# Gated attention and SwiGLU on one core: scale arithmetic and weight copies to GpSimd, probability casts to ScalarE

## The chip, the core and the metric

The kernel runs on one core of a Trainium2 chip. The metric is device time in microseconds (us): three runs took 1774.62 to 1776.85, median 1776.02. Beside them there is one profiled execution, from which all rows come.

A core has five engines that matter here, each with a queue that it works through in order: TensorE (PE, with its weight loads PEld), VectorE (DVE), ScalarE (ACT), GpSimd (POOL) and SyncE (SP), which here issues the DMAs. They meet at semaphores. Matmul results lie in PSUM, in eight banks of 128 x 512 float32; everything else lies in SBUF.

## The reference

Two branches on the same input of 2048 rows and 576 columns are mixed by a gate:

```python
g = sigmoid((x * gate_w).sum(-1, keepdims=True))
a = A_ref(x, wq, wk, wv, wo, beta)                 # 32 heads of 18, 4 segments of 512 rows
b = (silu(x @ w_gate) * (x @ w_up)) @ w_down       # 576 -> 4608 -> 576
return g * a + (1 - g) * b
# inside A_ref, for each segment:
p = softmax(qs @ ks.T * scale + mask);  a_dot = p @ vs
a_mem = (phi(qs) @ M) / (phi(qs) @ z + 1e-6)       # memory of the segments before
o = sigmoid(beta) * a_mem + (1 - sigmoid(beta)) * a_dot
```

## The kernel before

**Stages.** First the attention's projections are made, segment by segment, with the memory terms (to 239 us in the trace). Then comes the feed-forward branch, in two *halves* of two segments each. A half goes through the 36 blocks of 128 hidden columns, f = 0 to 35; one block is called a *unit* here. Last, a tail mixes and projects (from about 1692 us).

**A unit.** Gate and up products of the block are made together by a scheme of seven products in place of eight: `seven(t, j)` issues seven matmuls of 128 x 512 (L1365, L1368), 49 a unit. ScalarE and VectorE combine their sums between them: L1444, L1447, L1454 and L1458 are copies by ScalarE, L1451 and L1459 additions by VectorE, L1461 and L1463 the SiLUs, L1469 and L1470 products that give the hidden values, L1243 and L1246 their split into two float16 parts. The three accumulators have one PSUM bank each (0, 1 and 2), so the fifth product, which adds on to the bank that L1451 reads, waits for L1451.

**Ticks.** Between the products `tick()` is called eight times, k = 0 to 7; ticks 5 and 6 follow each other with no product between them. A tick issues what is due (`defer(n, fn)` puts a small piece of work n ticks ahead; the pieces of the next block's weights, L358, L362, L366, are spread in this way), then down products and steps of attention by the table `SHARE`. The order of the program is the order of each queue: nothing is moved by a scheduler.

**Heavy units.** The down products are made for three blocks at a time (CH = 3), in the first unit of each group of three after the first group: f = 3, 6, ..., 33 of a half, called *heavy*. They are 16 groups of nine matmuls (L1144), in two PSUM banks in turn (3 and 4), each ended by VectorE (L1151, L1153), which multiplies by `inv[c]` and adds to `ya`. In half zero the steps of attention run in the heavy units alone, ten in each but the first, at ticks 2 to 7; in half one they run in all units. The two lighter units after a heavy one are called the second and the third.

**A step of attention** makes scores twice: by rows for the maxima (L882, then VectorE's L900, which reads a bank and writes a scratch tile `junk`), and by columns (L993), on which ScalarE does `exp` into `pe` (L997) and GpSimd masks the diagonal (L1005). Two steps later `pe` is split: L1092 casts it to float16 (`p1`, VectorE) and L1094 subtracts (`p2`, GpSimd). The value products (L1021, L1023) come later still. The tiles of PSUM for this come from `ts_tile`, three banks (5, 6, 7) in turn. In half one units of attention are made in a second way (`turned`), which has no L1092.

**Scales.** Everything is held in float16 pairs under scales that are powers of two, worked out in the kernel from sums of squares. `across` adds columns over partitions by a matmul against ones (L155). `grade` cuts at a floor and takes a power of two near the reciprocal root by two bit steps (L149, L151, L152).

- `weigh(i, t)` (L169 to L190) does so for four blocks of gate and up weights: 17 steps on VectorE, 19 for i < 2, on operands of one to eight columns. It gives `sw`, `iw`, `hk`, `ha`, `hb`. For i = 0 and 1 it runs in the first part, for i = 2 to 8 at tick 2 of a third unit.
- `d_scale(c)` (L1106 to L1120) does it for three blocks of down weights: eight or nine steps on VectorE and one or two multiplications on GpSimd (L1119). It runs at tick 0 of the second unit.
- `d_look(f)` (L1104) gives it the sums: ScalarE squares a down weight block and writes the squares to `junk` too. `d_load` brings the blocks in ticks 0 to 2 of the first unit of the three, `d_look` follows at ticks 4 to 6.
- `d_split(f)` (L1122 to L1129) makes three float16 copies of a block: the scaled one (ScalarE, L1125), the rest (VectorE, L1126), and the first one divided by 2048 (VectorE, L1127), and stores them for half one.

`exp_table` (L1358) is a tiny `exp` that makes ScalarE load its table early, after the SiLUs.

Of the kernel before, what the change touches and what calls it, by code (L numbers as in the profile page):

```python
# [17 lines left out]
AF = mybir.ActivationFunctionType  # L18
# [51 lines left out]
def gated_mix(ctx, tc, xT, xrest, wf, wfr, wfh, wd, wv, wo, beta, cmask, ident, bmask, out):  # L70
# [77 lines left out]
    def grade(out, t, low=FLOOR):  # L148
        nc.vector.tensor_scalar_max(out, t, low)  # L149
        bits = out.bitcast(I32)  # L150
        nc.vector.tensor_scalar(bits, bits, 24, 127, op0=OP.logical_shift_right, op1=OP.bitwise_xor)  # L151
        nc.vector.tensor_single_scalar(bits, bits, 23, OP.logical_shift_left)  # L152

# [15 lines left out]
    def weigh(i, t):  # L169
        c = 20 + 9 * i  # L170
        n = 9 if i < 2 else 8
        e, z, m = sc[:, 0:8], column(8), sc[:, 9:13]
        across(t[:, :n], sc[:, c:c + n])
        nc.vector.tensor_reduce(sw[i], t[:, :n], axis=AX.X, op=OP.add)
        grade(sw[i], sw[i])
        nc.vector.tensor_scalar_mul(sw[i], sw[i], TOP)
        nc.vector.tensor_scalar(e, t[:, 0:8], sw[i], sw[i], op0=OP.mult, op1=OP.mult)
        if i < 2:
            nc.vector.tensor_scalar(z, t[:, 8:9], sw[i], sw[i], op0=OP.mult, op1=OP.mult)
            nc.vector.tensor_scalar_add(e, e, z)  # L180
        v = e.rearrange("p (f u) -> p f u", u=2)
        nc.vector.tensor_mul(m, v[:, :, 0], v[:, :, 1])
        nc.vector.tensor_reduce(z, m, axis=AX.X, op=OP.max)
        nc.vector.tensor_mul(z, z, xq)
        grade(z, z, 2.0 ** 26)
        nc.vector.tensor_mul(iw[i], sw[i], sx)
        nc.vector.tensor_scalar(hk[i], z, 4.0 * STEP * TOP, iw[i], op0=OP.mult, op1=OP.mult)
        nc.vector.tensor_scalar(ha[i], hk[i], iw[i], 1.0 / STEP, op0=OP.mult, op1=OP.mult)
        nc.vector.reciprocal(hb[i], ha[i])
        nc.vector.reciprocal(iw[i], iw[i])  # L190
# [192 lines left out]
    with ExitStack() as st:  # L383
# [344 lines left out]
        for s in range(NSEG):  # L728
            upd = upd_gen(s - 1) if s else None
            casts = []  # L730
            for n, (m, u) in enumerate(chains):
# [18 lines left out]
                if s == 2:  # L750
                    if n == 6:
                        mid.append(lambda: weigh(1, lone_tile([P, 9])))
                    if n == 0:
# [40 lines left out]
            for n in range(8):  # L794
# [4 lines left out]
                if s == 1:  # L799
                    if n == 3:  # L800
                        power(sx, lone_tile([P, 1]))
                    if n == 4:
                        reach(lone_tile([P, 4 * NT]))
                    if n == 6:
                        weigh(0, lone_tile([P, 9]))
# [30 lines left out]
    with ExitStack() as st:  # L836
# [205 lines left out]
        def att_gen():  # L1042
            N = 10 * NB
            for tau in range(N + TL + VL + 5):
# [44 lines left out]
                if 0 <= z < N and z // 5 not in turned:  # L1089
                    pe = cur.pop(z)  # L1090
                    p1 = ap.tile([P, L], F16, name="p1", bufs=6)
                    nc.vector.tensor_copy(p1, pe)  # L1092
                    p2 = ap.tile([P, L], F16, name="p2", bufs=6)
                    nc.gpsimd.tensor_sub(p2, pe, p1)  # L1094
                    cur["p", z] = (p1, p2)
# [10 lines left out]
        def d_scale(c):  # L1106
            t, r = ts_tile([P, CH]), sc[:, 13:16]
            across(t, sc[:, 123:126])
# [8 lines left out]
            nc.vector.tensor_reduce(inv[c], r, axis=AX.X, op=OP.min)  # L1117
            for n, i in enumerate(at):
                nc.gpsimd.tensor_mul(column(121 + n), inv[c], hb[i])  # L1119
            nc.vector.reciprocal(inv[c], inv[c])  # L1120

        def d_split(f, r):  # L1122
# [4 lines left out]
            defer(3, lambda: nc.vector.tensor_scalar_mul(d[:, 2], d[:, 0], 1.0 / STEP))  # L1127
# [111 lines left out]
        later = [False]  # L1239
        yas = {}  # L1240
# [132 lines left out]
        for pos, (half, f) in enumerate(seq):  # L1373
# [22 lines left out]
            if half == 0 and pos % 3 == 2 and 2 <= i < FT // 4:  # L1396
                plan.append((2, lambda i=i: weigh(i, ts_tile([P, 8]))))
# [15 lines left out]
            def tick():  # L1413
# [5 lines left out]
                if half == 0:  # L1419
                    if q == 0 and k < CH:  # L1420
                        draw[f + k] = d_load(f + k)
                    if q == 0 and 4 <= k < 4 + CH:
                        d_look(f + k - 4)
                    if q == 1 and k == 0:
                        d_scale(f // CH)
                    if (q, k) in ((1, 1), (1, 7), (2, 5)):
                        g = f - 1 if k == 1 else f
# [8 lines left out]
            later[0] = half == 1 and f > 0  # L1436
            ops, rem = wops.pop((half, f)), rhs[f % 2]
# [151 lines left out]
```

## Time and profile before

| What | Value |
|---|---|
| Median of three runs | 1776.02 us |
| Profiled execution, its own time | 1776.07 us |
| Its span, first to last instruction | 1774.4 us |
| Granted TensorE clock, mean | 0.996 |
| DMA, mean | 175 GB/s |
| First part; half zero; half one; tail (us) | 239.4; 736.8; 716.3; 81.9 |

The span is 1.7 us shorter than the execution's time, which lies 0.05 us off the median, so a microsecond in the trace is taken as one in the result. The page gives busy times of each engine. A row of a timeline reads: start, duration, engine, line, operation, out<-in, shapes, count, and in brackets the idle time of the engine before it and what ended that. A row of waits reads: who waited at which line, for what, us in total, times, longest. A row of stretches gives the stretch, its length, and then the busy time of PE, PEld, DVE, ACT and POOL with counts, the granted clock, and the DMA. Matmuls overlap one another, so a row's duration is longer than the time to the next start.

### The profile page before, as it was taken

What the parts mean: (1) busy time and instruction counts of PE and PEld (TensorE: products, weight loads), DVE (VectorE), ACT (ScalarE), POOL (GpSimd) and SP (SyncE); (2) the same over time, 40 slices, a digit from 0 to 9 for tenths busy, and PEclk for the clock granted to TensorE, in tenths of its full rate; (3) what the DMA queues carried; (4) which work ended last, traced back from release to release, by engine and by line L of the source; (5) the groups of instructions that cost most, each with busy time, mean ns of one, the idle gap of its engine ahead of it and who ended that gap; (6) DMA issues with size and microseconds to landing.
All of it is one profiled execution on the core that took longest, in us unless ns stands there. A gap on an engine that the chain in (4) does not pass through costs nothing.

```text
span 1774.4 us, 35271 instructions
## 1 busy us (share of the span) xinstructions
PE 1688.2 (95%) x12267; PEld 1094.0 (62%) x12267; DVE 1392.2 (78%) x3467; ACT 1047.0 (59%) x1868; POOL 839.5 (47%) x1083
## 2 busy tenths in 40 slices
PE   9999989999999999889899999999999999999999
PEld 7888855445555555555555566566556656655599
DVE  7788667888898889888887787878778788786565
ACT  7656567676766676566555656655664665565411
POOL 3325551246356544644552474656555565554121
PEclk9999999999999999999999999999999999999999
DMA  8656666656765674455444557764866586665544
GB/s 288 212 211 219 225 212 217 206 165 180 230 209 157 204 223 154 134 165 179 118 125 158 156 128 155 199 158 124 189 177 137 151 214 165 142 147 142 155 148 141
DMA packets 341670, 311.30 MB, mean 175 GB/s; under 512 B 193396, under 2 KB 258676, under 8 KB 341492
## 3 DMA queue, kind: packets, MB, share of 16 engines
q1 hardware_dynamic: 341492, 309.05, 60.6%
q8 instruction: 96, 1.57, 0.4%
q14 instruction: 82, 0.67, 0.1%
HBM read 183.20 MB, written 99.55 MB: 159 GB/s over the span
## 4 chain that ended last, share of the span: by engine, by line
PE 55%; DVE 18%; ACT 10%; issue 9%; DMA 5%; POOL 3%; SPq 1%; DVEq 0%; ACTq 0%; POOLq 0%
PE bank L1365 20%; PE bank L1144 16%; PE bank L212 7%; PE bank L1368 3%; PE bank L882 3%; PE bank L993 2%; DVE ya L1153 2%; ACT L1461 2%; DVE junk L900 2%; DVE hl L1246 1%; DMA rc<-rt 1%; PE bank L1021 1%; ACT row L1463 1%; ACT L1358 1%; DVE p L1092 1%
## 5 line engine op out<-in xcount | busy, mean ns | idle before, releaser
L1144 PE MATMUL bank<-dw,hh 128*128 128x320 f16 (+1 forms) x2304 | 436.9, 286 | 25.9 <-DVE ya L1153 21.3
L1144 PE MATMUL bank<-dw,hl 128*128 128x320 f16 (+1 forms) x1152 | 329.9, 286 | 1.1 <-DVE hl L1246 1.1
L1094 POOL TENSOR_TENSOR p<-pe,p 128x512 f16<-128x512 f32 x220 | 270.8, 1231 | 86.6 <-DVE p L1092 62.5
L1144 PEld LDWEIGHTS <-hh 128*128 128x128 f16 x2304 | 224.5, 98 | 117.1 <-issue 31.3
L997 ACT ACTIVATE pe<-bank 128x512 f32<-128x512 f32 x220 | 130.1, 591 | 194.4 <-PE bank L993 183.0
L1153 DVE SCALAR_TENSOR_TENSOR ya<-bank,sc,ya 128x320 f32<-128x320 f32 x352 | 176.0, 511 | 60.9 <-PE bank L1144 58.5
L900 DVE CUSTOM_DVE_ANT_0 junk<-bank,cm 128x128 bf16<-128x128 f32 (+2 forms) x352 | 169.5, 481 | 32.6 <-ACT junk L1104 22.2
L1368 PE MATMUL bank<-xr,rh 128*128 128x512 f16 x504 | 191.4, 380 | 0.4 <-DMA rh<-rc 0.4
L1005 POOL TENSOR_SCALAR_AFFINE_SELECT pe<-pe 128x256 f32<-128x256 f32 (+1 forms) x220 | 91.8, 417 | 175.1 <-ACT pe L997 171.3
L1246 DVE SCALAR_TENSOR_TENSOR hl<-hh,row 128x512 f16<-128x512 f16 x144 | 124.1, 862 | 27.1 <-ACT hh L1243 27.0
L358 POOL TENSOR_TENSOR ws<-raw 128x256 f32<-128x256 f32 x72 | 66.3, 921 | 152.0 <-DMA raw<-in_wf_dram 104.5
L882 PE MATMUL bank<-kst,qst 108*128 108x512 bf16 (+3 forms) x512 | 124.6, 299 | 12.5 <-ACT pe L997 10.9
L1144 PEld LDWEIGHTS <-hl 128*128 128x128 f16 x1152 | 112.5, 98 | 30.8 <-DVE hl L1246 1.8
L1092 DVE CAST p<-pe 128x512 f16<-128x512 f32 x220 | 110.1, 501 | 0.0
L1454 ACT ACTIVATE row<-bank 128x512 f32<-128x512 f32 x72 | 43.0, 597 | 103.8 <-PE bank L1368 103.8
L993 PE MATMUL bank<-qst,kst 111*128 111x512 bf16 (+3 forms) x352 | 103.3, 300 | 0.6 <-DMA kst<-stw 0.6
L1458 ACT ACTIVATE bank<-bank 128x512 f32<-128x512 f32 x72 | 41.9, 582 | 100.2 <-PE bank L1368 98.3
L1459 DVE TENSOR_TENSOR row<-bank,row 128x512 f32<-128x512 f32 x72 | 49.7, 690 | 56.2 <-ACT bank L1458 55.9
L212 PE MATMUL bank<-xo,qhi 128*128 128x512 f32 x288 | 92.6, 402 | 0.1
L1243 ACT ACTIVATE hh<-row 128x512 f16<-128x512 f32 x144 | 89.1, 619 | 5.0 <-DVE row L1469 4.1
L456 POOL TENSOR_TENSOR q<-qr,q 128x512 bf16<-128x512 f32 x36 | 47.9, 1332 | 84.6 <-ACT q L455 75.6
L1469 DVE SCALAR_TENSOR_TENSOR row<-bank,sc,row 128x512 f32<-128x512 f32 x72 | 53.8, 748 | 42.4 <-ACT row L1461 20.5
(1089 smaller groups left out, 4195.7 us busy)
## 6 DMA issues: line engine op xcount, KB each, us to landing
xo<-in_wf_dram SPq DMA_DIRECT2D x65, 320.0 KB
raw<-in_wf_dram SPq DMA_DIRECT2D x72, 256.0 KB
dc<-dw SPq DMA_DIRECT2D x36, 432.0 KB
dw<-dc SPq DMA_DIRECT2D x36, 432.0 KB
rh<-rc SPq DMA_DIRECT2D x72, 168.0 KB
draw<-in_wd_dram SPq DMA_DIRECT2D x36, 288.0 KB
xo<-in_xT_dram SPq DMA_DIRECT2D x33, 256.0 KB
vd<-vps SPq DMA_DIRECT2D x8, 912.0 KB
```

The source lines that it names most:

```text
L212: nc.tensor.matmul(t, st[n], mv[n], start=(n == 0), stop=(n == 13))
L882: nc.tensor.matmul(t[:, c:c + w], qs[:KR, pr, P * i:P * i + P], ks[:KR, pr, 0:w], start=True, stop=True)
L900: nc.vector.tensor_tensor_reduce(junk.bitcast(BF)[:, :w], t[:, c:c + w], cm[:, L - w:L], 1.0, -3.0e38, OP.add, OP.max, m[:, k:k + 1])
L993: nc.tensor.matmul(t[:, c:c + w], ks[:KR + 3, pr, P * j:P * j + P], qs[:KR + 3, pr, P * j:L], start=True, stop=True)
L997: nc.scalar.activation(pe, t, AF.Exp, scale=SCALE)
L1092: nc.vector.tensor_copy(p1, pe)
L1094: nc.gpsimd.tensor_sub(p2, pe, p1)
L1144: nc.tensor.matmul(t, p, d[:, q, cs], start=(f == CH * c and n == 0), stop=(f == CH * c + CH - 1 and n == 2))
L1153: nc.vector.scalar_tensor_tensor(ya[:, i, cs], t, inv[c], ya[:, i, cs], op0=OP.mult, op1=OP.add)
L1246: nc.vector.scalar_tensor_tensor(lo, hi, -STEP, src, op0=OP.mult, op1=OP.add)
L1365: nc.tensor.matmul(t, w[:, p, z], x[z][:, q], start=first and n == 0, stop=False, skip_group_check=True)
L1368: nc.tensor.matmul(t, rem[:, RPOS[j]], XR[j], start=False, stop=True, skip_group_check=True)
```

## The change

Five things, all in the first part and in half zero, with the first unit of half one.

1. `weigh` keeps five steps on VectorE (a copy out of PSUM, the sum, `grade`); seven, or eight for i < 2, go to GpSimd. The two bit steps of its second grading and two last multiplications become `reckon(i)`, the two reciprocals `back(i)`. In half zero they run at ticks 1, 5 and 8 (tick 0 of the next unit); in the first part one product or chain earlier than before, with `reckon` and `back` behind.
2. `d_scale` keeps `grade` on VectorE, the rest goes to GpSimd, its reciprocal becomes `d_back(c)`. From the second group on it runs at tick 5 of the heavy unit, `d_back` at tick 3 of the second unit. The first group's runs at tick 6 of f = 1, its reciprocal at tick 3 of f = 2.
3. `d_look` runs at ticks 2 to 4 of the heavy unit (the first group's at ticks 3 to 5 of f = 1). Two of the three blocks are loaded in the third unit before (ticks 2 and 4), the last at tick 0 of the heavy unit. The first group's splits come at ticks 1, 3 and 5 of f = 2; the others' places stay.
4. The third copy of `d_split` goes to GpSimd.
5. The cast L1092 goes to ScalarE in half zero for two of every five steps before f = 24 and for all from f = 24 on, and in the first unit of half one.

```diff
+    def halve(out):
         bits = out.bitcast(I32)
         nc.vector.tensor_scalar(bits, bits, 24, 127, op0=OP.logical_shift_right, op1=OP.bitwise_xor)
         nc.vector.tensor_single_scalar(bits, bits, 23, OP.logical_shift_left)
+
+    def grade(out, t):
+        nc.vector.tensor_scalar_max(out, t, FLOOR)
+        halve(out)
...
     def weigh(i, t):
...
+        e, z = sc[:, 0:n], column(9)
+        g = nc.gpsimd
         across(t[:, :n], sc[:, c:c + n])
+        nc.vector.tensor_copy(e, t[:, :n])
         nc.vector.tensor_reduce(sw[i], t[:, :n], axis=AX.X, op=OP.add)
         grade(sw[i], sw[i])
+        g.tensor_scalar_mul(sw[i], sw[i], TOP)
+        g.tensor_scalar(e, e, sw[i], sw[i], op0=OP.mult, op1=OP.mult)
         if i < 2:
+            g.tensor_scalar_add(e[:, 0:8], e[:, 0:8], e[:, 8:9])
+        v = e[:, 0:8].rearrange("p (f u) -> p f u", u=2)
+        g.tensor_mul(v[:, :, 0], v[:, :, 0], v[:, :, 1])
+        m = [e[:, 2 * k:2 * k + 1] for k in range(4)]
+        g.tensor_scalar(z, m[0], m[1], m[2], op0=OP.max, op1=OP.max)
+        g.tensor_scalar(z, z, m[3], xq, op0=OP.max, op1=OP.mult)
+        g.tensor_scalar_max(z, z, 2.0 ** 26)
+        g.tensor_mul(iw[i], sw[i], sx)
+
+    def reckon(i):
+        z, g = column(9), nc.gpsimd
+        halve(z)
+        g.tensor_scalar(hk[i], z, 4.0 * STEP * TOP, iw[i], op0=OP.mult, op1=OP.mult)
+        g.tensor_scalar(ha[i], hk[i], iw[i], 1.0 / STEP, op0=OP.mult, op1=OP.mult)
+
+    def back(i):
         nc.vector.reciprocal(hb[i], ha[i])
         nc.vector.reciprocal(iw[i], iw[i])
...
-                    nc.vector.tensor_copy(p1, pe)
+                    if later[0] or z % 5 not in turn_of[0]:
+                        nc.vector.tensor_copy(p1, pe)
+                    else:
+                        nc.scalar.activation(p1, pe, AF.Copy)
...
         def d_scale(c):
             t, r = ts_tile([P, CH]), sc[:, 13:16]
             across(t, sc[:, 123:126])
             grade(r, t)
-            nc.vector.tensor_scalar_mul(r, r, TOP)
+            g.tensor_scalar_mul(r, r, TOP)
...
-                nc.vector.tensor_scalar(z, z, ha[i], 2.0 ** 100, op0=OP.mult, op1=OP.min)
-            nc.vector.tensor_reduce(inv[c], r, axis=AX.X, op=OP.min)
+                g.tensor_scalar(z, z, ha[i], 2.0 ** 100, op0=OP.mult, op1=OP.min)
+            g.tensor_scalar(inv[c], r[:, 0:1], r[:, 1:2], r[:, 2:3], op0=OP.min, op1=OP.min)
...
-            defer(3, lambda: nc.vector.tensor_scalar_mul(d[:, 2], d[:, 0], 1.0 / STEP))
+            defer(3, lambda: nc.gpsimd.tensor_scalar_mul(d[:, 2], d[:, 0], 1.0 / STEP))
...
-                    if q == 0 and k < CH:
-                        draw[f + k] = d_load(f + k)
-                    if q == 0 and 4 <= k < 4 + CH:
-                        d_look(f + k - 4)
-                    if q == 1 and k == 0:
-                        d_scale(f // CH)
+                    g = {(0, 0): f + 2, (2, 2): f + 1, (2, 4): f + 2}.get((q, k), FT) if f > 1 else k if f == 0 and k < CH else FT
+                    if g < FT:
+                        draw[g] = d_load(g)
+                    if (f == 1 and 3 <= k < 3 + CH) or (f > 1 and q == 0 and 2 <= k < 2 + CH):
+                        d_look(k - 3 if f == 1 else f + k - 2)
+                    if (f, k) == (1, 6) or (f > 1 and (q, k) == (0, 5)):
+                        d_scale(f // CH)
+                    if (f, k) == (2, 3) or (f > 2 and (q, k) == (1, 3)):
+                        d_back(f // CH)
...
+            turn_of[0] = (1, 3) if pos < 24 else (0, 1, 2, 3, 4)
```

More of the change, by code (lines that the diff above doesn't have):

```diff
@@ L803, in gated_mix @@
                         reach(lone_tile([P, 4 * NT]))
+                    if n == 5:
+                        weigh(0, lone_tile([P, 9]))
                     if n == 6:
-                        weigh(0, lone_tile([P, 9]))
+                        reckon(0)
+                    if n == 7:
+                        back(0)
                 if s:
@@ L1239, in gated_mix @@
         later = [False]
+        turn_of = [()]
         yas = {}
```

31 lines of the change are left out of this document (11 added, 20 removed).

## The prediction

> **What bounds the kernel now.** I read the page's busy times first, then the busy times by stage (the first attention part, half zero, half one, the tail), then the list of waits of TensorE alone.
>
> ```profile
> PE 1688.2 (95%) x12267; PEld 1094.0 (62%) x12267; DVE 1392.2 (78%) x3467; ACT 1047.0 (59%) x1868; POOL 839.5 (47%) x1083
> ```
> ```profile
> 0.00:239.40 239.40, 225.91 (x1293) 196.84 (x1294) 177.73 (x432) 148.62 (x296) 104.28 (x119) 0.99 0.67 227
> 239.40:976.20 736.80, 674.92 (x4578) 393.11 (x4579) 612.82 (x1456) 477.34 (x861) 338.78 (x443) 0.99 0.58 179
> 976.20:1692.50 716.30, 708.95 (x5791) 428.33 (x5790) 555.99 (x1493) 410.31 (x684) 381.43 (x502) 1.00 0.65 159
> ```
> ```profile
> PE bank L1144 <- DVE ya L1153: 21.3, 25, 2.1
> PE bank L1365 <- DVE bank L1451: 18.8, 22, 1.7
> PE bank L882 <- ACT pe L997: 10.9, 12, 1.2
> PE bank L155 <- ACT junk L1104: 4.5, 1, 4.5
> ```
>
> TensorE is busy all but 86.2 us (1774.4 less 1688.2). No edit shortens a matmul, so only that idle time can be won. Of it 61.9 us lie in half zero (736.80 less 674.92), 13.5 us in the first part and only 7.4 us in half one, which the change hardly touches. The waits say who ends the idle time: VectorE (DVE) for 21.3 + 18.8 us, ScalarE's (ACT) `exp` for 10.9 us, one stop of 4.5 us at a scale's column sum. The change lightens VectorE in just these stages; the question is how much of each wait was caused by the work that goes.
>
> **Part 1, `d_scale` leaves the second unit of each group of three.** Nine such units, by their busy times (span, PE, PEld, DVE, ACT, POOL), the first and the sum; then VectorE's scale, from its second step to its last, and TensorE, in the first of them.
>
> ```profile
> 433.14:445.48 12.34, 10.88 (x53) 5.01 (x51) 11.63 (x25) 7.82 (x13) 7.38 (x10) 1.00 0.45 123
> ...
> sum 110.36, PE 97.88 PEld 45.08 DVE 103.64 ACT 70.40 POOL 68.43; mean PE 10.88 PEld 5.01 DVE 11.52 ACT 7.82 POOL 7.60
> ```
> ```profile
> 435.24 0.17 DVE L151 TENSOR_SCALAR sc<-sc 128x3 int32<-128x3 int32 x1
> 435.45 1.02 DVE L152 TENSOR_SCALAR sc<-sc 128x3 int32<-128x3 int32 x1
> ...
> 437.43 0.16 DVE L1120 RECIPROCAL sc<-sc 128x1 f32<-128x1 f32 x1 [0.30 <-POOL sc L1119]
> ```
> ```profile
> 440.95 0.59 PE L1365 MATMUL bank<-xo,wo__5001 128*128 128x512 f16 x2 [1.46 <-DVE bank L1451]
> ```
>
> Nine units lose 12.48 us (110.36 less 97.88), 1.39 each; a tenth of the kind (f = 7), outside the view, I put at the same, together 13.9. VectorE is busy 94% of these units, and the add L1451, which frees the bank that the fifth product needs, stands behind the scale. From its second step to its end the scale holds the queue from 435.24 to 437.59, 2.35 us, more than the 1.46 us that TensorE waits. All of it goes: the three grading steps move to the heavy unit, the reciprocal behind L1451. What is late next is L1451's own bank and the product before it, which nothing delays. I take 12 us, bounds 6 (half the slack refilled) and 13.9.
>
> **Part 2, the heavy units.** Sums of five heavy units before f = 24, and of the four from f = 24, then the two places that recur.
>
> ```profile
> sum 185.41, PE 176.04 PEld 118.64 DVE 150.80 ACT 126.20 POOL 98.91; mean PE 35.21 PEld 23.73 DVE 30.16 ACT 25.24 POOL 19.78
> ```
> ```profile
> sum 158.04, PE 141.73 PEld 94.90 DVE 136.37 ACT 86.27 POOL 86.41; mean PE 35.43 PEld 23.73 DVE 34.09 ACT 21.57 POOL 21.60
> ```
> ```profile
> 420.46 0.29 DVE L900 CUSTOM_DVE_ANT_0 junk<-bank,cm 128x128 bf16<-128x128 f32 x1 [2.27 <-ACT junk L1104]
> ```
> ```profile
> 421.68 0.27 PE L882 MATMUL bank<-kst,qst 108*128 108x256 bf16 x1 [1.20 <-ACT pe L997]
> ```
> ```profile
> 741.29 0.27 PE L1144 MATMUL bank<-dw,hh 128*128 128x256 f16 x1 [1.48 <-DVE ya L1153]
> ```
> ```profile
> L1243 ACT ACTIVATE hh<-row 128x512 f16<-128x512 f32 x144 | 89.1, 619 | 5.0 <-DVE row L1469 4.1 <-DVE row L1470 0.8
> L1461 ACT ACT_TABLE_LOAD x59 | 75.7, 1283 | 1.0
> ...
> L1104 ACT ACTIVATE junk<-draw 128x576 f16<-128x576 f32 x36 | 24.3, 675 | 12.7 <-DVE mb L900 8.8 <-issue 2.0 <-DMA draw<-in_wd_dram 1.9
> ```
> ```profile
> L1092 DVE CAST p<-pe x40: 382/422/842, 711.4 to 932.3; 128x512 f16<-128x512 f32 x40
> ```
>
> The squares L1104 write the same scratch tile as VectorE's maxima L900, so the square of tick 5 makes VectorE stand 2.27 us, and it stands in ScalarE's queue between two table loads ahead of the `exp` for which TensorE then waits 1.20 us. Two ticks earlier it meets neither: VectorE gets 2.27 us back, and ScalarE 0.68 us and a read of the sum before that `exp`. Against it ScalarE takes casts of 0.62 us (row L1243, same shape, a bound either side of little width). Before f = 24 four of ten go over, one of them just before the table load, so the wait of 1.20 us loses only some 0.1 us; VectorE's three grading steps, 0.5 to 1.3 us, fill the stand that goes. Of 9.37 us idle in five units I take 2.5 and for f = 6 another 0.5. From f = 24 all forty casts go, 0.42 us each by their median, 4.2 us a unit on a VectorE busy 86%. Waits like the one at 741.29, behind a run of casts at the unit's end, go; those ahead of the casts stay. Of 16.31 us I take 7. Bounds of this part: 0 and 18.
>
> **Part 3, `weigh` in the third unit.** Sum of five units that hold one; its first and last step; the wait behind it.
>
> ```profile
> sum 59.64, PE 55.24 PEld 24.66 DVE 52.44 ACT 46.94 POOL 19.56; mean PE 11.05 PEld 4.93 DVE 10.49 ACT 9.39 POOL 3.91
> ```
> ```profile
> 452.80 0.15 DVE L174 TENSOR_REDUCE sc<-bank 128x1 f32<-128x8 f32 x1
> ...
> 455.86 0.14 DVE L190 RECIPROCAL sc<-sc 128x1 f32<-128x1 f32 x1
> ```
> ```profile
> 456.44 0.39 PE L1365 MATMUL bank<-xo,wo__5230 128*128 128x512 f16 x1 [0.49 <-DVE wo__5230 L366]
> ```
>
> Seventeen steps, 3.1 us, shrink to five at tick 1 (0.19 us apart, some 0.95 us), two at tick 5 and two at tick 8. L366 comes 2 us sooner and its wait goes. But the five now stand ahead of L1451, where a third copy (0.30 to 0.83 us) goes away: about even. Of 4.40 us I take 2.5, and 0.5 for the units without a `weigh`; bounds 0 and 5.
>
> **Part 4, the first attention part.** The wait of the value products, and the same twelve matmuls undisturbed.
>
> ```profile
> 158.30 1.83 PE L212 MATMUL bank<-vw,xo 128*128 128x288 f32 x12
> ...
> 163.63 3.17 PE L212 MATMUL bank<-vw,xo 128*128 128x288 f32 x12 [2.57 <-DVE r L476]
> ```
> VectorE's first step of block 1's `weigh` stands in this row:
>
> ```profile
> 147.88 0.16 DVE L174 TENSOR_REDUCE sc<-bank 128x1 f32<-128x9 f32 x1
> ```
>
> From there it has hardly a gap to the place of the wait, 15 us later. Ten of its nineteen steps leave, some 0.2 us each as in the third unit, and it starts a chain earlier, into idle time. The wait of 2.57 us and the slow matmuls after it (3.17 less 1.83) make 3.9; I take 3.5, bounds 0 and 3.9. Block 0's `weigh` one value product earlier finds its bank free, but the next value product wants the same bank and waits for the two reads instead: nothing won.
>
> **Part 5, the first chunk's scale.** The 4.5 us at L155 look won, since unit 0 no longer squares. But in unit 1 the last square is queued at tick 5 and the column sum follows at tick 6, with no product between. ScalarE must first do a table load of 1.28 us, two SiLUs and two squares there; TensorE waits nearly as long as now. I take 1 us, bounds -1 and 6.
>
> **Part 6, GpSimd (POOL).** It gets 125 single-column steps and 36 copies. A row of GpSimd's timeline, then two groups of its instructions:
>
> ```profile
> 435.29 1.15 POOL L1094 TENSOR_TENSOR p<-pe,p 128x512 f16<-128x512 f32 x1
> ```
> ```profile
> L1119 POOL TENSOR_TENSOR sc<-sc 128x1 f32<-128x1 f32 x18 | 3.1, 190 | 44.8 <-DVE sc L1117 44.8
> ...
> L601 POOL CAST bm<-xo 128x456 bf16<-128x456 f32 (+1 forms) x2 | 1.0, 495 | 0.0
> ```
> A step is 0.19 us; a copy of 576 columns lies between L601's 0.50 us and the 1.15 us of the two-input subtraction (L1094), and as one-input work I take 0.6: 46 us on an engine busy 47%, which TensorE does not wait for. The loads of the down weights leave SyncE's queue (SP) thinner at the heavy unit's start: two go out in the unit before, one waits there for the last chunk's split on VectorE. Behind it in that queue stand the unit's weight loads, each needed a unit later, so I take nothing. VectorE's two steps of `reckon` wait for GpSimd's seven of `weigh` (1.3 us), but stand four ticks behind. For `reckon`, `back` and the three crowded splits in unit 2 I give back 4 us, bounds 0 and 12.
>
> On the port: L152 took 1.02 us at 435.45, L151 before it, the same form, 0.17 us; the subtraction L1094 of the row above held GpSimd from 435.29 to 436.44, when L152 ended too (436.47). [...]
>
> **Sum.** 12 + 3 + 7 + 3 + 3.5 + 1 - 4 = 25.5 us off the profiled execution's 1776.07 us (span 1774.4), which lies on the median of 1776.02. That is 1750.5 us.
>
> **Rivals.** *VectorE is blocked by GpSimd.* If each of 36 copies and 9 `weigh`s holds a VectorE step that TensorE waits for by 0.25 us or more, some 12 us come back: 1763. [...] *GpSimd's order turns on the kernel* (slower). Its steps of `d_scale` wait for VectorE in front of the mask (L1005) and the subtraction; if VectorE is late by over some 5 us, two steps of attention, ScalarE's cast waits for the mask, the next `exp` stands behind it, and TensorE loses it. At 3.6 us in each of ten heavy units the 25.5 turn into +10.5: 1786.5. Against it: GpSimd is idle 17 us of 37 in a heavy unit. *More goes than I count*: the other waits of the heavy units and the stop in unit 1 as well, 10 us: 1740. *The scale is not what holds L1451*, and the other steps fill its place: within 3.5 us of now, 1775.
>
> **Chances.** Forecast (1745 to 1758) 0.57, blocked VectorE 0.19, more 0.10, nothing 0.05, slower 0.09. The range from 1738 to 1768 leaves out the slower case, nothing, and a little of both ends. A measurement here tells some 0.2% from no change, 3.5 us. Faster 0.86, same 0.05, slower 0.09.
>
> **What would show it.** Right: the second units last 10.9 to 11.1 us and the wait at L1451 there is gone; VectorE has no stand of 2 us on L1104's scratch in heavy units, and the wait at L882 is still near 1 us; the wait at 163.6 is gone; the one at L155 in unit 1 is still 3 to 5 us. Wrong: L1451 is late in the second units behind stretched L322 and L366; ScalarE idle on GpSimd's mask; TensorE's idle time in half zero over 45 us.

## The result, and the profile after

The changed kernel took 1759.51 us (median of four runs, 1755.72 to 1760.99) against 1776.29 us of the kernel before (four runs): a ratio of 0.9904, 95% interval 0.9887 to 0.9921. It is 16.8 us faster, where 25.5 had been forecast. Its profiled execution took 1758.92 us, with a span of 1757.2.

The same views as before, of the changed kernel. First the page's busy times, then the stretches of the first part, half zero and half one (length, then busy time of PE, PEld, DVE, ACT, POOL), then four rows of TensorE's waits:

```profile
PE 1689.3 (96%) x12267; PEld 1096.2 (62%) x12267; DVE 1331.4 (76%) x3248; ACT 1079.2 (61%) x1933; POOL 946.8 (54%) x1244
```
```profile
0.00:241.78 241.78, 228.06 (x1293) 198.30 (x1294) 172.99 (x412) 148.97 (x297) 111.41 (x139) 0.99 0.66 225
241.78:958.17 716.39, 673.94 (x4578) 394.01 (x4579) 555.61 (x1260) 507.53 (x923) 437.88 (x584) 0.99 0.59 184
958.17:1675.27 717.10, 708.82 (x5791) 428.14 (x5788) 556.97 (x1490) 411.95 (x687) 382.31 (x502) 1.00 0.64 158
```
```profile
PE bank L1169 <- DVE ya L1178: 15.9, 19, 2.8
PE bank L1391 <- ACT bank L1474: 12.4, 9, 1.6
PE bank L901 <- ACT pe L1016: 7.2, 10, 0.9
PE bank L158 <- ACT junk L1126: 4.0, 1, 4.0
```

(L1169, L901 and L158 are L1144, L882 and L155 of before; L1391, L1394, L1474 and L1481 are L1365, L1368, L1444 and L1451; L369, L373 and L377 are the sums, high and low parts of the weights, L358, L362 and L366 of before.) Half zero is 20.4 us shorter (736.80 to 716.39). TensorE's wait for VectorE's L1451, 18.8 us before, is down to 1.2. A wait that was hardly there (0.8 us, once) has grown: TensorE waits nine times for ScalarE's copy L1474, 12.4 us in all.

By kind of unit, the sums of the changed kernel: nine second units, five third units, five heavy units (f = 9 to 21), and the four heavy units from f = 24:

```profile
sum 95.20, PE 95.20 PEld 43.12 DVE 79.18 ACT 72.47 POOL 76.55; mean PE 10.58 PEld 4.79 DVE 8.80 ACT 8.05 POOL 8.51
```
```profile
sum 53.87, PE 53.87 PEld 25.07 DVE 38.57 ACT 33.49 POOL 33.75; mean PE 10.77 PEld 5.01 DVE 7.71 ACT 6.70 POOL 6.75
```
```profile
sum 191.63, PE 177.77 PEld 119.70 DVE 150.41 ACT 148.79 POOL 127.72; mean PE 35.55 PEld 23.94 DVE 30.08 ACT 29.76 POOL 25.54
```
```profile
sum 160.46, PE 145.76 PEld 96.97 DVE 130.98 ACT 106.68 POOL 101.45; mean PE 36.44 PEld 24.24 DVE 32.74 ACT 26.67 POOL 25.36
```

The light units are won whole: the sum of the stretches equals TensorE's busy time (95.20 and 95.20), so it never stands there, where before nine second units took 110.36 us and five third units 59.64. The heavy units went the other way, 185.41 to 191.63 and 158.04 to 160.46, though 10 us had been forecast for them.

The place of the loss is the border of a third and a heavy unit. Here is that at 454.35 us in GpSimd's timeline (start, duration), where `weigh` of the change stands, then in ScalarE's and in TensorE's:

```profile
446.00 2.27 POOL L1152 TENSOR_SCALAR dw<-dw 128x576 f16<-128x576 f16 x1 [3.82 <-ACT dw L1150]
449.22 0.23 POOL L181 TENSOR_SCALAR sc<-sc 128x1 f32<-128x1 f32 x1 [0.95 <-DVE sc L151]
449.56 0.85 POOL L182 TENSOR_SCALAR sc<-sc 128x8 f32<-128x8 f32 x1
...
452.15 0.19 POOL L191 TENSOR_TENSOR sc<-sc 128x1 f32<-128x1 f32 x1
452.30 0.73 POOL L369 TENSOR_TENSOR ws<-raw 128x256 f32<-128x256 f32 x1
453.11 1.05 POOL L369 TENSOR_TENSOR ws<-ws,raw 128x256 f32<-128x256 f32 x1
```
```profile
454.19 0.72 ACT L373 ACTIVATE wo__5295<-ws,sc 128x512 f16<-128x512 f32 x1 [2.03 <-POOL ws L369]
...
457.40 1.28 ACT L1384 ACT_TABLE_LOAD   x1
...
458.80 0.58 ACT L1474 ACTIVATE bank<-bank 128x512 f32<-128x512 f32 x1
```
```profile
459.43 1.46 PE L1391 MATMUL bank<-xo,wo__5295 128*128 128x512 f16 x6 [1.61 <-ACT bank L1474]
```

From 449.22 to 452.30 GpSimd does the seven small steps of `weigh`, on one to eight columns (3.1 us). Behind them in its queue are the sums of the next block's weights, L369. ScalarE stands 2.03 us for these, in front of two SiLUs, two weight copies, a table load and L1474. The third product of the unit, which adds on to the bank that L1474 reads, starts 1.61 us late (the expectations below speak of the fourth). One such row stands in each of the seven heavy units that follow a `weigh`. Nothing of this waits for the result of `weigh`; it only stands behind it.

### The profile page after: what moved, and what is told of

Same layout as the page of the kernel before. It is cut to its first block, busy times and chain, and to the rows that moved or that the text cites. A ratio compares the mean times of both kernels' runs of the same rounds, so it can differ in the third digit from the quotient of the medians.

```text
span 1757.2 us, 35261 instructions
## 1 busy us (share of the span) xinstructions
PE 1689.3 (96%) x12267; PEld 1096.2 (62%) x12267; DVE 1331.4 (76%) x3248; ACT 1079.2 (61%) x1933; POOL 946.8 (54%) x1244
## 4 chain that ended last, share of the span: by engine, by line
PE 63%; ACT 11%; DVE 11%; issue 5%; POOL 4%; DMA 4%; SPq 1%; DVEq 0%; ACTq 0%; POOLq 0%
PE bank L1391 25%; PE bank L1169 18%; PE bank L223 7%; PE bank L1394 4%; PE bank L901 3%; PE bank L1012 2%; ACT L1491 2%; ACT L1384 1%; PE bank L1040 1%; ACT row L1491 1%; ACT row L1493 1%; ACT pe L1016 1%; POOL ws L369 1%; DVE ya L1178 1%; PE bank L974 1%
## 5 line engine op out<-in xcount | busy, mean ns | idle before, releaser
L1169 PE MATMUL bank<-dw,hh 128*128 128x320 f16 (+1 forms) x2304 | 436.8, 286 | 19.5 <-DVE ya L1178 15.9
L1169 PE MATMUL bank<-dw,hl 128*128 128x320 f16 (+1 forms) x1152 | 329.5, 286 | 0.8 <-DVE hl L1272 0.8
L1116 POOL TENSOR_TENSOR p<-pe,p 128x512 f16<-128x512 f32 x220 | 268.1, 1219 | 55.5 <-DVE p L1112 36.1
L1169 PEld LDWEIGHTS <-hh 128*128 128x128 f16 x2304 | 224.5, 98 | 107.4 <-issue 25.3
L1016 ACT ACTIVATE pe<-bank 128x512 f32<-128x512 f32 x220 | 130.1, 592 | 180.5 <-PE bank L1012 156.4
L1178 DVE SCALAR_TENSOR_TENSOR ya<-bank,sc,ya 128x320 f32<-128x320 f32 x352 | 177.7, 512 | 59.7 <-PE bank L1169 57.8
L1394 PE MATMUL bank<-xr,rh 128*128 128x512 f16 x504 | 191.4, 380 | 0.8 <-DMA rh<-rc 0.8
L901 PE MATMUL bank<-kst,qst 108*128 108x512 bf16 (+3 forms) x512 | 124.7, 299 | 9.7 <-ACT pe L1016 7.2
L1169 PEld LDWEIGHTS <-hl 128*128 128x128 f16 x1152 | 112.4, 98 | 30.5 <-DVE hl L1272 1.5
L1152 POOL TENSOR_SCALAR dw<-dw 128x576 f16<-128x576 f16 x36 | 79.8, 2216 | 76.8 <-ACT dw L1150 76.7
L1499 DVE SCALAR_TENSOR_TENSOR row<-bank,sc,row 128x512 f32<-128x512 f32 x72 | 53.9, 749 | 47.6 <-PE bank L1394 26.2
L1394 PEld LDWEIGHTS <-rh 128*128 128x128 f16 x504 | 49.4, 98 | 60.9 <-issue 1.8
```

What stands on the lines that cost most here:

```text
L901: nc.tensor.matmul(t[:, c:c + w], qs[:KR, pr, P * i:P * i + P], ks[:KR, pr, 0:w], start=True, stop=True)
L1016: nc.scalar.activation(pe, t, AF.Exp, scale=SCALE)
L1169: nc.tensor.matmul(t, p, d[:, q, cs], start=(f == CH * c and n == 0), stop=(f == CH * c + CH - 1 and n == 2))
L1178: nc.vector.scalar_tensor_tensor(ya[:, i, cs], t, inv[c], ya[:, i, cs], op0=OP.mult, op1=OP.add)
L1394: nc.tensor.matmul(t, rem[:, RPOS[j]], XR[j], start=False, stop=True, skip_group_check=True)
```

## Experiments

**The theory** from these rows: the loss lies in GpSimd's order, `weigh`'s steps and the third copies (2.27 us each) standing ahead of the sums. **The rival**: VectorE is held by GpSimd, as it may be at 435.45 in the kernel before (L152 took 1.02 us, L151 ahead of it 0.17), by the amount of GpSimd's work, and the place does not matter. A second doubt is whether the casts on ScalarE win what they were priced at. All kernels in one table: medians and ratios to the kernel before, then from each profiled execution half zero and the sums for the same units as above (us).

| Kernel | Median | Ratio, 95% interval | Half zero | Heavy 9 to 21 | Heavy 24 to 33 | Nine second | Five third |
|---|---|---|---|---|---|---|---|
| before | 1776.3 | | 736.8 | 185.4 | 158.0 | 110.4 | 59.6 |
| the change | 1759.5 | 0.9904 (0.9887 to 0.9921) | 716.4 | 191.6 | 160.5 | 95.2 | 53.9 |
| `weigh` a unit earlier | 1760.6 | 0.9916 (0.9899 to 0.9932) | 717.6 | 180.9 | 157.9 | 95.8 | 65.6 |
| `weigh` on VectorE | 1767.2 | 0.9957 (0.9941 to 0.9973) | 725.8 | 181.3 | 158.3 | 95.2 | 73.5 |
| third copies on VectorE | 1758.7 | 0.9911 (0.9896 to 0.9926) | 722.0 | 191.1 | 160.9 | 95.2 | 53.6 |
| casts on VectorE | 1754.2 | 0.9881 (0.9865 to 0.9897) | 714.5 | 189.2 | 158.4 | 95.2 | 53.9 |
| moves only | 1759.0 | 0.9903 (0.9889 to 0.9916) | 717.5 | 182.3 | 162.2 | 95.2 | 58.3 |
| `d_scale` on VectorE | 1762.2 | 0.9921 (0.9908 to 0.9934) | 720.1 | 191.0 | 164.7 | 95.2 | 53.9 |
| `weigh` cut in two | 1746.3 | 0.9830 (0.9816 to 0.9843) | 701.3 | 181.6 | 157.3 | 95.2 | 53.9 |
| cut, casts on VectorE | 1741.1 | 0.9804 (0.9789 to 0.9819) | 698.9 | 179.4 | 156.4 | 95.2 | 53.9 |
| the same, first part too | 1740.4 | 0.9804 (0.9784 to 0.9824) | 699.0 | 179.3 | 156.5 | 95.2 | 53.9 |

**`weigh` a unit earlier.**

```diff
-            if half == 0 and pos % 3 == 2 and 2 <= i < FT // 4:
+            if half == 0 and pos % 3 == 1 and 2 <= i < FT // 4:
                 plan += [(1, lambda i=i: weigh(i, ts_tile([P, 8]))), ...
```

> The changed kernel, but the later groups' `weigh`, `reckon` and `back` are issued one unit earlier, in the second unit of a group of three (same engines, same instructions). Theory (GpSimd's order: the seven single-column steps of `weigh` stand ahead of the block sums L369 at the end of the third unit, ScalarE waits 2 us for these sums, and its copy L1474 and TensorE's fourth product are late by 1.8 us in the heavy unit): the wait of TensorE at L1391 for ScalarE's L1474 (12.4 us in 9) falls under 3 us, the seven heavy units that follow a `weigh` lose 1.5 to 1.8 us each, and the kernel takes 1747 to 1750 us, about 0.984 of the kernel before, unless VectorE's few steps in the second unit cost up to 2 us there. [...]

TensorE's waits of this kernel:

```profile
PE bank L1391 <- ACT row L1493: 10.7, 7, 1.8
PE bank L1391 <- ACT bank L1474: 5.2, 9, 1.0
```

The heavy units fell by 10.8 us as the theory said, and the rival, which had them keep their length within 0.5 us each (and the kernel at 1757 to 1761 us), fell. But the time stayed: the third units got 11.8 us longer. A wait of up to 1.8 us, once for each of seven `weigh`s, moved with it by one unit, now for ScalarE's SiLU L1493; and 5.2 us of waits for L1474 are left, where under 3 were expected. ScalarE's row shows the same cause in front of it, in the second unit:

```profile
440.95 0.72 ACT L373 ACTIVATE wo__5185<-ws,sc 128x512 f16<-128x512 f32 x1 [2.25 <-POOL ws L369]
```

The sums L369 stand behind `weigh` in either unit. The expected time missed because a unit earlier is not a place free of sums.

**`weigh` on VectorE.**

```diff
 def weigh(i, t):
-        g = nc.gpsimd
+        g = nc.gpsimd if i < 2 else nc.vector
 def reckon(i):
-        z, g = column(9), nc.gpsimd
+        z, g = column(9), nc.gpsimd if i < 2 else nc.vector
```

> The changed kernel, but in the later groups the arithmetic of `weigh` and `reckon` runs on VectorE, at the ticks of the change. Theory (GpSimd's order): GpSimd reaches the block sums L369 some 3 us earlier, TensorE's wait for L1474 falls under 3 us as with the earlier `weigh`; VectorE has nine more steps of 0.15 to 0.2 us in the third unit, ahead of the add that frees a bank, so third units get back 0.5 to 1.4 us of the 1.9 us each that they won. In all 1750 to 1756 us. [...]

```profile
PE bank L1391 <- DVE bank L1481: 16.2, 9, 2.2
...
PE bank L1391 <- ACT bank L1474: 1.5, 3, 0.8
```

The wait for L1474 went, by its cause. The price on VectorE was mis-sized: the five third units got 19.6 us longer (53.9 to 73.5), 3.9 each and not 0.5 to 1.4. TensorE in one of them, and that unit as a stretch:

```profile
449.83 2.32 PE L1391 MATMUL bank<-xo,wo__5202 128*128 128x512 f16 x6 [2.13 <-DVE bank L1481]
```
```profile
441.35:456.04 14.69, 12.56 (x52) 5.43 (x51) 10.80 (x27) 9.09 (x17) 5.11 (x5) 0.88 0.81 285
```

Seven of the nine steps stand ahead of the add L1481 on VectorE, which is busy 10.59 us in such a unit where it was 7.71, and TensorE stops for 2.13. After the stop its matmuls are slow: six took 2.32 us in place of 1.46, the granted clock of each of the five units is 0.88 where it was 1.00, and TensorE is busy 62.78 us in them in place of 53.87. So 8.9 of the 19.6 us are slower matmuls. The rival's time (1760 to 1770 us) came out, without its reason: the heavy units were to keep their length and did not (191.6 to 181.3).

**Third copies on VectorE.**

```diff
-            defer(3, lambda: nc.gpsimd.tensor_scalar_mul(d[:, 2], d[:, 0], 1.0 / STEP))
+            defer(3, lambda: nc.vector.tensor_scalar_mul(d[:, 2], d[:, 0], 1.0 / STEP))
```

> The changed kernel, but the third copy of the down weights (L1152, 2.27 us each on GpSimd) is back on VectorE (0.3 us and more there). Theory (GpSimd's order): one of the three copies of a group is issued at the end of the third unit and stands with `weigh` ahead of the block sums; without its 2.27 us GpSimd has caught up, and TensorE's wait for L1474 falls from 12.4 to between 0 and 6 us; VectorE gains 36 copies of some 0.3 to 0.5 us, which cost up to 4 us in second and third units. In all 1748 to 1757 us. [...]

The copies in the groups of instructions of this kernel (duration minimum, median, maximum in ns), and its wait:

```profile
L1152 DVE TENSOR_SCALAR dw<-dw x36: 295/299/830, 275.7 to 942.6; 128x576 f16<-128x576 f16 x36
```
```profile
PE bank L1391 <- ACT bank L1474: 12.8, 9, 1.8
```

Both fell, the rival with the 1 us or more that it gave each of the ten heavy units (1745 to 1752 us). GpSimd lost 36 copies (its busy time in half zero fell from 437.88 to 366.71 us), and the wait stayed at 12.8 us: the copies are no part of the cause, since `weigh` waits for VectorE's L151 anyway and the copy ahead of it is done by then. The heavy units kept their length (191.1 and 160.9) though GpSimd worked 19.6 us less in these nine, so the amount of its work does not set their length either. On VectorE the copies cost 5.6 us of half zero in the profiled execution, 3.0 of it from block 35 on; the medians do not tell the two kernels apart.

**Casts on VectorE.**

```diff
-            turn_of[0] = (1, 3) if pos < 24 else (0, 1, 2, 3, 4)
+            turn_of[0] = ()
```

> The changed kernel, but all casts of the probabilities in half zero are on VectorE again. The casts were priced to win 7 us in the heavy units from block 24 on. Theory: the waits that remain in the late heavy units are of VectorE (the down products' bank, 15.9 us in all), so without ScalarE's casts the four late units lose 3 to 7 us together and the six early ones 0 to 3: 1762 to 1769 us. Rival (ScalarE's added casts are what makes its L1474 late, 0.62 us each in its queue): the wait for L1474 falls by half and the kernel gets faster by 2 to 6 us: 1753 to 1757 us.

```profile
PE bank L1169 <- DVE ya L1178: 17.1, 23, 1.8
PE bank L1391 <- ACT bank L1474: 13.0, 10, 1.6
...
PE bank L901 <- ACT pe L1016: 3.6, 10, 0.4
```

Taken back, the casts make the kernel faster: the intervals of the two ratios overlap (0.9887 to 0.9897), but its slowest run, 1755.03 us, is below the changed kernel's fastest, 1755.72. So the theory's price was wrong in sign; so was the rival's mechanism, for the wait for L1474 stayed. What fell is the wait for the `exp` L1016, 7.2 to 3.6 us: on ScalarE a cast stands ahead of an `exp`. Half zero of the two profiled executions differs by 1.9 us only, so the traces place less than half of the 5.3 us between the medians.

In the four late heavy units the 2.1 us are all in that of block 27; the other three together are 0.9 us shorter with the casts on ScalarE. Here it is with them (first row) and without, then a step of VectorE and one of GpSimd in the changed kernel:

```profile
755.45:798.05 42.60, 38.46 (x308) 24.92 (x307) 33.53 (x77) 26.55 (x48) 24.86 (x35) 0.92 0.37 103
```
```profile
753.76:793.40 39.64, 35.50 (x309) 23.92 (x307) 36.54 (x85) 21.94 (x39) 25.18 (x35) 1.00 0.38 108
```
```profile
783.01 1.10 DVE L927 CAST mq<-mr 128x8 bf16<-128x8 f32 x1
```
```profile
782.92 1.17 POOL L1116 TENSOR_TENSOR p<-pe,p 128x512 f16<-128x512 f32 x1
```

The longest wait for VectorE, 2.8 us with and 1.8 without, is in this unit. VectorE has less to do there with the casts on ScalarE, but L927 took 1.10 us and ends with GpSimd's subtraction L1116, which runs beside it. With the casts on VectorE the cast that the subtraction needs stands behind this step in VectorE's own queue; in the kernel with the cut and those casts, below, the step took 0.17 us at this place (765.65) and the cast began at 766.19. But TensorE's idle time in the unit is 4.14 us both times: the 3.0 us are its slower matmuls, busy 38.46 us in place of 35.50 at a granted clock of 0.92 in place of 1.00. Units 0 to 8, on the other hand, were 2.6 us longer without the casts on ScalarE (155.60 against 153.00).

**Moves only**: the kernel before with `d_load`, `d_look`, `d_scale` and the splits of the first chunk at the new places and the reciprocal by itself; all arithmetic, third copies and casts on VectorE. Beside the new schedule in `tick` (as in the change) the edit is:

```diff
 def d_scale(c):
+        g = nc.vector
-            nc.vector.tensor_reduce(inv[c], r, axis=AX.X, op=OP.min)
+            g.tensor_scalar(inv[c], r[:, 0:1], r[:, 1:2], r[:, 2:3], op0=OP.min, op1=OP.min)
+        def d_back(c):
             nc.vector.reciprocal(inv[c], inv[c])
```

> The kernel before with one part of the change alone: loads, squares and scale of the down weights at their new places, the reciprocal by itself, the splits of the first chunk one unit later; all arithmetic of `weigh`, the scale, the third copies and the casts on VectorE as before. Theory (the gain is from the moves: the scale and its column sum leave the second unit): second units 10.6 to 11.2 us each, so 12 to 16.7 us are won there, third units keep about 11.9, heavy units gain some from the earlier squares: 1752 to 1763 us. Rival (the gain is from taking single-column work and third copies off VectorE): second units stay above 11.6 us and the kernel above 1768 us.

Sums of nine second and five third units:

```profile
sum 95.17, PE 95.17 PEld 43.17 DVE 93.10 ACT 70.43 POOL 72.69; mean PE 10.57 PEld 4.80 DVE 10.34 ACT 7.83 POOL 8.08
```
```profile
sum 58.32, PE 55.22 PEld 24.67 DVE 51.74 ACT 46.93 POOL 19.36; mean PE 11.04 PEld 4.93 DVE 10.35 ACT 9.39 POOL 3.87
```

The second units are won by the moves alone, with VectorE still busy 93.10 us of 95.17. And the kernel takes 1758.96 us, as long as the whole change: the work for GpSimd and ScalarE as it was placed brought nothing in all. It won in third units (58.3 to 53.9) and in small amounts elsewhere what it lost in the early heavy ones (182.3 to 191.6).

**`d_scale` on VectorE**: in the changed kernel, `g = nc.vector` in `d_scale`.

> The changed kernel, but the single-column arithmetic of the down weights' scale runs on VectorE, at the place of the change in the heavy unit. Theory: those five or six steps on GpSimd are at the unit's middle, where GpSimd has idle time, so they neither win nor lose: heavy units within 0.4 us, 1757 to 1762 us. Rival (any single-column step on GpSimd delays the masks and subtractions behind it): heavy units 0.5 to 1 us shorter, 1749 to 1755 us.

The early heavy units did not move (191.0), but the late ones got 4.2 us longer, 3.3 of it in the unit of block 30, with 26.6 us of waits for VectorE's L1178 in place of 15.9. "Neither wins nor loses" fell for the late units: there TensorE waits longer for VectorE's adds. The 4.2 us are not all their price: in the unit of block 30, 1.0 us of the 3.3 are slower matmuls (granted clock 0.96, in the change 1.00), and the medians, 1762.2 and 1759.5, have intervals that overlap.

**`weigh` cut in two.** GpSimd's steps but the first go behind the sums; engines and instructions stay.

```diff
+    def rate(i):               # GpSimd's steps of weigh but the first
...
-  plan += [(1, lambda i=i: weigh(i, ...)), (5, lambda i=i: reckon(i)), (8, lambda i=i: back(i))]
+  plan += [(1, lambda i=i: weigh(i, ...)), (9, lambda i=i: rate(i)), (11, lambda i=i: reckon(i)), (12, lambda i=i: back(i))]
```

> The changed kernel, but the later groups' `weigh` is cut in two: the column sum, VectorE's five steps and GpSimd's first step stay in the third unit; GpSimd's other steps come in the heavy unit, behind the block sums L369, with `reckon` and `back` behind them. Same instructions on the same engines, only their order on GpSimd is another. Theory (order on GpSimd alone): the wait for L1474 falls under 3 us, the seven heavy units from block 6 to 24 last 36.2 us or less (39.1 in that of block 24), and the third units stay at 10.6 to 10.8 us, because nothing stands ahead of the sums any more: 1746 to 1749 us. Rival (the sum of GpSimd's work, wherever it stands, is what takes the time): as with the earlier `weigh`, the wait turns up elsewhere, in the masks and subtractions of the heavy unit and so in the `exp` and the value products: 1756 to 1761 us.

GpSimd at the same border in this kernel (L376 are the sums), TensorE's wait for the copy (L1481 here), and half zero:

```profile
444.35 0.23 POOL L181 TENSOR_SCALAR sc<-sc 128x1 f32<-128x1 f32 x1 [0.96 <-DVE sc L151]
444.66 0.72 POOL L376 TENSOR_TENSOR ws<-raw 128x256 f32<-128x256 f32 x1
445.46 1.06 POOL L376 TENSOR_TENSOR ws<-ws,raw 128x256 f32<-128x256 f32 x1
```
```profile
PE bank L1398 <- ACT bank L1481: 1.7, 3, 0.8
```
```profile
240.72:942.05 701.33, 669.20 (x4579) 392.99 (x4579) 557.89 (x1260) 507.08 (x923) 441.60 (x583) 1.00 0.61 188
```

The sums follow `weigh`'s first step at once. GpSimd is as busy as before the cut (441.60 against 437.88 us), and in the five early heavy units even busier (135.14 against 127.72); yet these are 10.1 us shorter, half zero is 15.1 us shorter, no new wait takes the place, and third units stay at 53.87. This decides it: the order, not the amount. By the medians the cut is worth 13.2 us; some 2 of the 15.1 are the unit of block 27, whose granted clock is 1.00 here and was 0.92.

**Cut, and the casts on VectorE from block 6 on.**

```diff
-            turn_of[0] = (1, 3) if pos < 24 else (0, 1, 2, 3, 4)
+            turn_of[0] = (1, 3) if pos < 6 else ()
```

> The same cut `weigh`, and the casts of the probabilities on ScalarE only before block 6, on VectorE from there on. Theory (two separate losses of the change, 12 us from `weigh`'s order and 3 to 5 us from the casts): they add, heavy units from 6 to 21 together 212 to 215 us, from 24 on 154 to 157 us, and the kernel takes 1740 to 1745 us, less than both kernels. Rival (the casts were a loss only because ScalarE was late behind `weigh`): without the late L1474 the casts on VectorE win nothing or cost what was priced, so it takes 1747 us or more.

The two losses add: 1741.1 us against 1746.3, heavy units shorter by 2.2 and 0.9 us, the 0.9 again in that of block 27 (40.64 to 39.59, here with the clock at 1.00 both times). The two intervals just meet (0.9816 and 0.9819). Against the kernel before and the changed one it is well clear, 35 us and 18 us.

**The first part too**: the same cut for `weigh(1)` in the first attention part.

```diff
                 if s == 2:
                     if n == 5:
                         mid.append(lambda: weigh(1, lone_tile([P, 9])))
-                    if n == 7:
-                        mid.append(lambda: reckon(1))
-                    if n == 8:
-                        mid.append(lambda: back(1))
...
                 if s == 3:
+                    if n in (0, 2, 3):
+                        mid.append(lambda fn={0: rate, 2: reckon, 3: back}[n]: fn(1))
```

> The kernel with the cut `weigh` and the casts on VectorE from block 6 on, and in the first attention part `weigh` of block 1 cut in the same way: GpSimd's seven steps behind its first one, `reckon` and `back` come in the next segment, where GpSimd has gaps of 2 to 3 us. Theory (order on GpSimd again: in the kernel with block 1's `weigh` on GpSimd, VectorE waits 3.7 us for the memory sums Mm of L542, which stand behind it): that wait falls under 1.5 us, the value product that waits 2.7 us for `r` of L494 starts 2 to 3 us earlier, the first part is some 3 us shorter and the kernel takes 1736 to 1740 us. Rival (VectorE is held there by ScalarE and its own queue, as it was in the kernel before): the wait for Mm goes, but the value product still waits over 2 us, and the time stays at 1740 to 1743 us.

VectorE's wait for the memory sums in the changed kernel and in this one, then the value product in this one:

```profile
156.36 0.78 DVE L534 TENSOR_TENSOR mtmp<-bank,bm 128x152 f32<-128x152 f32 x2 [3.69 <-POOL Mm L535]
```
```profile
152.62 0.32 DVE L541 TENSOR_TENSOR mtmp<-bank,bm 128x152 f32<-128x152 f32 x1 [1.64 <-POOL Mm L542]
```
```profile
161.72 1.86 PE L230 MATMUL bank<-vw,xo 128*128 128x288 f32 x12 [0.89 <-DVE r L494]
```

The wait for Mm fell to 1.64 us (under 1.5 was expected), and the value product starts 2.75 us earlier than in the kernel without this edit (164.47) after a wait of 0.89 in place of 2.67. The first part took 236.22 us in the profiled execution against 239.27. The medians, 1740.37 and 1741.09, do not show it; so the mechanism is shown in the trace and the gain in the result is not.

## Why the prediction was right, and which step failed

The direction and the range held. The sum was 8.7 us too good, and it came from terms that missed both ways, so the range held in part by luck. The span fell by 17.2 us: 20.4 in half zero, less 2.4 in the first part and 0.8 in half one. Of the 20.4, 15.2 and 5.8 come from the nine second and five third units, -8.6 from the nine heavy ones, and 8.1 from units outside these views (3.7 in units 0 to 8, 4.4 in the third units from block 26 on and at the end of the half), of which the forecast named about 3.

- **Part 1, second units** (12 us forecast): right in its mechanism, and too small. Nine units gave 15.2 us (110.36 to 95.20), more than their idle time of 12.48: TensorE's busy time fell too, 97.88 to 95.20. Two things make up the 2.7 us. The column sum itself left these units, 0.15 us of TensorE each (434.65 to 434.80 in the first), and went to the heavy ones. And part of a stop counts as busy, since the last matmul ahead of it shows its full length (0.38 us for 128 x 512) and not the time to the next start (0.22). So 13.9, drawn from idle time, was no upper bound. That the moves alone do it is shown.
- **Part 3, third units** (3 us): five gave 5.8 us, again with less busy time (55.24 to 53.87). The moves give 1.3 of it, the work taken off VectorE 4.5.
- **Part 2, heavy units** (10 us): the term that failed. Five and four of them got 6.2 and 2.4 us longer. Its first link held: VectorE's waits for the scratch tile of the squares, the next row in the kernel before, fell to 0.4 us, once. The working followed VectorE and ScalarE through the heavy unit and took the stalls as gone; it did not ask what GpSimd's new steps do to the sums of the block that comes next.

```profile
DVE junk L900 <- ACT junk L1104: 22.2, 11, 2.3
```

- **Part 6 is the step at fault.** It named who waits for the *results* of `weigh` ("two steps of `reckon` ... but stand four ticks behind") and took GpSimd's work as one "which TensorE does not wait for". What stands *behind* `weigh` in GpSimd's queue, the sums L369, was left out. With only that order cured, the kernel is 13.2 us faster; of the 4 us given back in that part, none was for this. Its price of a third copy, 0.6 us, was wrong as well (2.27 us), and there it made no difference.
- **The casts** (they were to give the 7 us in the late heavy units): not won. The wait for VectorE's down products is 15.9 us with them on ScalarE and 17.1 without. In the five early units they cost 2.4 us with the order as in the change and 2.2 with the cut; in the late ones 2.1 and 0.9, all in the unit of block 27. The row that spoke against them was shown in the prediction, the `exp` for which TensorE waits: 10.9 us before, 7.2 in the change, 3.6 without the casts on ScalarE. For the early units a cast was set against it; for the late ones only VectorE's relief was counted.
- **Part 4, the first part** (3.5 us): not won. The wait at the value product is 2.66 us where it was 2.57. VectorE came free earlier and then stood 3.69 us for GpSimd, behind the eight steps of `weigh(1)`; in the last experiment, with seven of them moved, the product starts 2.75 us earlier. And 1.3 us of the 3.9 that were counted are slow matmuls, which stood behind this wait in three executions of ten (last section). That this part of the changed kernel took 241.78 us and not 239.40 is scatter: seven other executions with the same first part took 238.84 to 240.72.
- **Part 5, unit 1** (1 us): the wait fell from 4.5 to 4.0 us, as argued.
- **The signs.** The waits at L1451 in second units and on the scratch tile are gone, the wait at L882 is 0.9 us at most, and that at L155 is 4.0 us, as named. The second units last 10.6 us, less than the 10.9 to 11.1 named. The wait at 163.6 was to go and did not. TensorE's idle time in half zero is 42.5 us; over 45 was named as a sign of being wrong.

**The rivals.** "VectorE is blocked by GpSimd" came near in time (1763) and is wrong as the main cause: 19.6 us of GpSimd's work taken out of the heavy units changed them by no more than 0.5 us, and with the cut `weigh` they were shorter with more of it. Single rows show a VectorE step that lasts until GpSimd's step beside it ends: L152 at 435.45 in the prediction, 1.02 us (to 436.47, GpSimd's to 436.44), and L927 at 783.01 above, 1.10 us (to 784.11, GpSimd's to 784.09). No run shows the port that the prediction names, nor the 0.25 us for each copy and each `weigh`, which was an estimate, and such rows give no price for the heavy units here. "GpSimd's order turns on the kernel" was the right mechanism at another place and with a smaller price: it put `d_scale` ahead of the masks, 36 us, where it was `weigh` ahead of the sums, some 13 us. Its chance of 0.09 was for a kernel slower than before, which did not come. With that cured and the casts back, heavy units are 6.0 and 1.6 us shorter than before. That is near the 9.5 us that Part 2 had forecast for them, but by luck in part: it had put 2.5 and 7, and the 7 were to come from casts that are on VectorE again here.

## What to carry to other kernels

When work goes to an engine that is idle half of the time, look at what stands behind it in that engine's queue, not only at who needs its result: seven steps of 0.2 to 0.9 us, with slack of a unit and more, cost some 13 us because the next block's sums came after them. Moving such a block earlier only moves the wait; putting it behind what is due at once removes it. And try the parts of a change alone: here the moves gave all of its gain, the offload nothing, and the offload in another order 13 us more (1759.0 to 1746.3).

## What the hardware showed that was not expected

A float16 copy with a factor, 128 x 576, took 2.27 us on GpSimd and 0.30 us on VectorE:

```profile
L1152 POOL TENSOR_SCALAR dw<-dw x36: 1647/2272/2298, 276.9 to 939.4; 128x576 f16<-128x576 f16 x36
```

GpSimd's copy took 7.6 times as long. GpSimd's steps on one to eight columns took 0.19 to 0.85 us in the rows above, VectorE's that write one column 0.14 to 0.16 in those of the prediction.

The length of a stop did not settle at which rate TensorE went on. The same twelve matmuls after the same wait, in the changed kernel and in the one with the earlier `weigh`:

```profile
165.54 3.09 PE L223 MATMUL bank<-vw,xo 128*128 128x288 f32 x12 [2.66 <-DVE r L487]
```
```profile
164.17 1.85 PE L223 MATMUL bank<-vw,xo 128*128 128x288 f32 x12 [2.65 <-DVE r L487]
```

The granted clock from 166 to 169 us is 0.50 in the first; in the second the next twelve, from 166.75, took 1.86 us. The twelve right behind this wait were slow in three of the ten executions in which the wait was 2.57 to 2.67 us (before, the change, casts on VectorE). In the unit of block 27 a stop of 2.80 us was followed by 6 us at a granted clock of 0.50 in the changed kernel (787.82 to 793.80), with the six matmuls of a product in 2.77 us in place of 1.46; with the cut `weigh`, where the longest wait for L1185 (L1178 of the change) is 2.8 us too, the granted clock of the unit is 1.00. With `weigh` on VectorE, slow matmuls followed the stop of 2.1 us in each of the five third units (granted clock 0.88).

Why matmuls were slow behind a stop in one execution and not in another, no run here shows.
